# HGRN2 attention and a three-way maxout FFN on one core: the first FFN group started on half of its tokens, with its first weights on GpSimd's queue

## The chip, the cores and the metric

One Trainium2 chip, one core of it. The metric is device time in microseconds for one execution of the whole kernel (attention and FFN in one program). Times are medians over several runs; the profile is of one further execution.

## The reference

The reference is two blocks in a row. The attention block is a gated linear recurrence over 768 time steps, for 4 batches of 8 heads of width 48; the FFN works on the 3072 resulting tokens of width 384.

```python
f = 1.0 / (1.0 + np.exp(-f_logit))
for t in range(S):                       # S = 768
    state = f[:, :, t, :, None] * state + np.einsum('bhd,bhe->bhde', k[:, :, t], v[:, :, t])
    y[:, :, t] = np.einsum('bhd,bhde->bhe', q[:, :, t], state)
x = y.transpose(0, 2, 1, 3).reshape(B * S, H * D)          # 3072 x 384
h = np.maximum(np.maximum(x @ w1, x @ w2), x @ w3)         # 384 -> 768, three times
out = h @ w_out                                            # 768 -> 384
```

q, k, v and f_logit are fp32. The four FFN weights are fp64 in the reference and reach the kernel as 64-bit words, so the kernel turns each weight into fp32 itself.

## The kernel before

**Attention.** The recurrence is cut into chunks of 64 steps. A unit `u` is one chunk of two batches, 128 tokens, and there are NU = 24 units; `u` and `u + 2` are successive chunks of the same two batches, with a carried state `st`. The work of a unit is split over small functions that the program calls in an order written out by hand:

- `sigmoids(u)`: f is transposed on TensorE (line 243) and ScalarE writes `gate` (line 260).
- `after(u)`: VectorE's backward scan of the gates gives `r` (line 282), k is transposed (line 243), `kh` = k times r (line 289); GpSimd keeps the chunk's total decay in `ends` (line 288).
- `before(u)`: the forward scan gives `prod` (line 296), q is transposed, `qh` = q times prod (line 300).
- `carry(u)`: GpSimd decays the old state (line 306).
- `keys(u)`: TensorE transposes `kh` (line 315), ScalarE copies it to `ks` (line 317).
- `pairs(u)`: the 64x64 scores (line 328), masked by VectorE into `at` (line 331).
- `values(u)`: scores times v (line 342), keys times v (line 351), and the new state `st` on VectorE (lines 357 and 359).
- `finish(u)`: the carried state's part (line 372); ScalarE copies the result into `heads` (line 378).

The first BY_ROWS = 8 units are loaded with tokens on partitions, two DMAs of 64 partitions for each of f, k, q and v (line 159); later ones in 32x32 blocks (line 174). Pads of the tiles have fixed values, for f the value GATE_PAD.

**From attention to FFN.** Four units are one group of 512 tokens. `heads` has a head on 48 of 64 partitions; `pack` (line 389) moves the heads to dense feature rows of `xT` with DMAs inside the chip, 10 for a range of units. It can use SyncE's queue alone (`one`) or SyncE's and ScalarE's in turn (`both`).

**FFN.** For each of NJ = 6 slices j of 128 hidden features and each of the three input weights i, three matmuls of 512 tokens (line 401) fill a PSUM tile `p` (two buffers, shared with `busy` and with some early transposes); i = 0 is copied by ScalarE into `top` (line 405), i = 1 and i = 2 are folded in by VectorE (line 407), the last one into `hm`. Then, for each 128 tokens, six matmuls of 384 columns with `w_out` (line 422), a ScalarE copy (line 427) and two output DMAs (line 431). There are six such groups. `ffn` is a generator: `fill(n)` runs n of its steps (18 and then 4 of them), and the program places these calls between the parts of the attention units, so that TensorE always has FFN matmuls to do in between.

**Weights.** The weights come as 24 pieces of 384 KB: 18 of w1, w2, w3 in the order j, i and six of w_out. `load_weights` (line 200) loads a piece into `raw`, which has 12 buffers. Each piece is converted in three stages: `round_begin` (ScalarE, lines 212 and 215), `round_middle` (VectorE, lines 224 and 225, then GpSimd, line 227) and `round_end` (VectorE, line 234). Five pieces are begun before the first group; during the first group each FFN step runs one or two more.

**The start.** The program loads units 0 to 3, works through their attention, packs all 512 tokens at once (`pack(0, GRP - 1, xT, both)`), and starts `ffn(0)`. `busy(n)` issues n matmuls of 256 columns whose results nobody reads (line 448); `busy(14)` stands between the last part of unit 3 and the first FFN matmul.

**The end.** A test that the fast path was numerically allowed (`least`, lines 578 to 582) is worked out during the last group, between two of its steps. If it fails, another path (`general`) runs; it doesn't run here.

## Time and profile before

| | us |
|---|---|
| median of 4 runs | 487.1 |
| lowest and highest | 486.51, 490.26 |
| the profiled execution: device time | 491.23 |
| the profiled execution: span from first to last instruction | 489.5 |
| mean granted TensorE clock in it | 0.985 of full |

| engine | busy us | share of the span |
|---|---|---|
| TensorE, matmul (PE) | 468.2 | 96% |
| TensorE, weight load (PEld) | 253.4 | 52% |
| VectorE (DVE) | 223.3 | 46% |
| ScalarE (ACT) | 109.3 | 22% |
| GpSimd (POOL) | 99.3 | 20% |

A line of the profile names the line of the kernel, the engine, the operation, `out<-in` with the program's tile names, and the shapes. SPq, ACTq and DVEq are the issuing of instructions by an engine's sequencer, DMAs above all. An fp32 matmul or weight load stands as two records, one for each of two passes. In a timeline, a start and a duration are followed by the number of records merged; in brackets stand the idle time of the engine just before and what ended it. In the row of 40 slices a digit is the busy share of a slice of 12.2 us in tenths. The profiled execution lies 0.85% above the median (491.23 against 487.1).

### The profile page before, as it was taken

What the parts mean: (1) busy time and instruction counts of PE and PEld (TensorE: products, weight loads), DVE (VectorE), ACT (ScalarE), POOL (GpSimd) and SP (SyncE); (2) the same over time, 40 slices, a digit from 0 to 9 for tenths busy, and PEclk for the clock granted to TensorE, in tenths of its full rate; (3) what the DMA queues carried; (4) which work ended last, traced back from release to release, by engine and by line L of the source; (5) the groups of instructions that cost most, each with busy time, mean ns of one, the idle gap of its engine ahead of it and who ended that gap; (6) DMA issues with size and microseconds to landing.
All of it is one profiled execution on the core that took longest, in us unless ns stands there. A gap on an engine that the chain in (4) does not pass through costs nothing.

```text
span 489.5 us, 10037 instructions
## 1 busy us (share of the span) xinstructions
PE 468.2 (96%) x4101; PEld 253.4 (52%) x4101; DVE 223.3 (46%) x346; ACT 109.3 (22%) x227; POOL 99.3 (20%) x132
## 2 busy tenths in 40 slices
PE   5879999998999999999999999999999999989994
PEld 4656455555554556554456554456554445434452
DVE  7954999993263461353462253471354420112110
ACT  2344445332122122122022122022121011100000
POOL 2122456553110220211220211210211300000000
PEclk9979999998999999999999999999999999999998
DMA  9898999633664032566033575023630012100002
GB/s 128 134 234 200 261 214 206 91 75 66 112 87 63 1 66 50 94 95 88 1 68 58 100 91 74 0 64 67 106 45 1 1 48 50 32 1 1 0 20 51
DMA packets 170007, 38.51 MB, mean 79 GB/s; under 512 B 154976, under 2 KB 168800, under 8 KB 169952
## 3 DMA queue, kind: packets, MB, share of 16 engines
q1 hardware_dynamic: 166208, 36.50, 41.7%
q10 hardware_dynamic: 3744, 1.28, 1.4%
q8 instruction: 34, 0.56, 0.5%
q14 instruction: 21, 0.17, 0.1%
HBM read 28.31 MB, written 4.72 MB: 67 GB/s over the span
## 4 chain that ended last, share of the span: by engine, by line
PE 86%; SPq 6%; DMA 3%; DVE 1%; issue 1%; ACT 1%; POOL 0%; ACTq 0%; DVEq 0%; POOLq 0%
PE p L401 55%; PE p L422 19%; SPq L159 3%; PE y L342 2%; PE y L372 2%; SPq L174 2%; DMA v_ld<-in_v_dram 2%; PE a L328 2%; PE p L448 2%; PE y L351 2%; PE tr L315 1%; DMA k_ld<-in_k_dram 1%; PE tr L243 1%; SPq L389 1%; SPq L200 1%
## 5 line engine op out<-in xcount | busy, mean ns | idle before, releaser
L401 PE MATMUL p<-xT,w_in 128*128 128x512 f32 x648 | 288.1, 596 | 0.7 <-ACT top L405 0.7
L401 PEld LDWEIGHTS p<-xT,w_in 128*128 128x128 f32 x648 | 120.0, 190 | 138.4 <-issue 132.3
L422 PE MATMUL p<-w_out,hm 128*128 128x384 f32 x288 | 98.3, 497 | 0.6 <-DVE w_out L234 0.6
L407 DVE TENSOR_TENSOR top<-p,top 128x512 f32<-128x512 f32 x36 | 24.7, 686 | 119.2 <-PE p L401 119.0
L422 PEld LDWEIGHTS p<-w_out,hm 128*128 128x128 f32 x288 | 54.6, 193 | 39.0 <-issue 4.1
L405 ACT COPY top<-p 128x512 f32<-128x512 f32 x36 | 21.1, 586 | 179.8 <-PE p L401 179.8
L407 DVE TENSOR_TENSOR hm<-p,top 128x512 f32<-128x512 f32 x36 | 24.8, 689 | 50.5 <-PE p L401 50.5
L288 POOL COPY ends<-r 128x8 f32<-128x8 f32 x24 | 4.6, 192 | 190.2 <-DVE r L282 190.1
L227 POOL TENSOR_TENSOR top_bits<-top_bits,rest_bits 128x384 uint32<-128x384 uint32 x24 | 28.2, 1175 | 40.5 <-DVE top_bits L225 23.9
L427 ACT COPY o<-p 128x384 f32<-128x384 f32 x24 | 11.4, 476 | 107.7 <-PE p L422 104.5
L296 DVE TENSOR_TENSOR_SCAN prod<-gate,from_inv 128x520 f32<-128x520 f32 x24 | 34.7, 1448 | 0.0
L282 DVE TENSOR_TENSOR_SCAN r<-gate,from_one 128x520 f32<-128x520 f32 x24 | 30.9, 1288 | 3.1 <-issue 2.3
L378 ACT COPY heads<-y 64x256 f32<-64x256 f32 (+1 forms) x72 | 26.5, 368 | 10.4 <-PE y L372 9.2
L331 DVE TENSOR_TENSOR at<-a,mask 128x512 f32<-128x512 f32 x24 | 16.5, 687 | 24.9 <-PE a L328 24.9
L300 POOL TENSOR_TENSOR qh<-qt,prod 128x512 f32<-128x512 f32 x16 | 18.8, 1175 | 39.0 <-DVE qt L247 39.0
L342 PEld LDWEIGHTS y<-at,v_ld 64*64 64x64 f32 x768 | 13.8, 134 | 17.9 <-issue 14.1
L289 POOL TENSOR_TENSOR kh<-kt,r 128x512 f32<-128x512 f32 x16 | 19.7, 1231 | 14.1 <-DVE kt L247 13.4
L317 ACT COPY ks<-tr 128x512 f32<-128x512 f32 x22 | 12.8, 582 | 39.2 <-PE tr L315 38.9
L306 POOL TENSOR_TENSOR state<-st,ends 128x384 f32<-128x384 f32 x22 | 20.3, 923 | 0.2
L342 PE MATMUL y<-at,v_ld 64*64 64x64 f32 x768 | 17.3, 224 | 2.5 <-DMA v_ld<-in_v_dram 2.2
L247 DVE STREAM_TRANSPOSE gate<-sig 128x512 f32<-128x512 f32 x16 | 11.3, 706 | 17.6 <-ACT sig L263 17.6
L359 DVE TENSOR_TENSOR st<-y,state 128x384 f32<-128x384 f32 x20 | 11.1, 555 | 14.0 <-PE y L351 13.8
(66 smaller groups left out, 289.5 us busy)
## 6 DMA issues: line engine op xcount, KB each, us to landing
raw<-in_moe_w_dram SPq DMA_DIRECT2D x18, 384.0 KB, 6.2
v_ld<-in_v_dram SPq DMA_DIRECT2D x48, 96.0 KB, 3.1
out_dram<-o SPq DMA_DIRECT2D x48, 96.0 KB, 2.2
raw<-in_moe_w_out_dram SPq DMA_DIRECT2D x6, 384.0 KB, 6.2
xT<-heads SPq DMA_DIRECT2D x30, 72.0 KB, 2.1
f_ld<-in_f_logit_dram SPq DMA_DIRECT2D x32, 64.0 KB, 2.7
k_ld<-in_k_dram SPq DMA_DIRECT2D x32, 64.0 KB, 2.6
q_ld<-in_q_dram SPq DMA_DIRECT2D x32, 64.0 KB, 2.5
```

The source lines that it names most:

```text
L227: nc.gpsimd.tensor_tensor(top, top, rest, op=ALU.add)
L282: nc.vector.tensor_tensor_scan(r[:, 0:LEN][:, ::-1], flat(gate)[:, ::-1], flat(from_one)[:, ::-1], 1.0, op0=ALU.mult, op1=ALU.max)
L289: (nc.vector if u < BY_ROWS else nc.gpsimd).tensor_tensor(kh.rearrange("p h a t -> p a h t"), kt, by_batch(r[:, 1:LEN + 1].rearrange("p (x ...
L296: nc.vector.tensor_tensor_scan(flat(prod), flat(gate_tiles[u % 2]), flat(from_inv[u % 2]), 1.0, op0=ALU.mult, op1=ALU.max)
L300: (nc.vector if u < BY_ROWS else nc.gpsimd).tensor_tensor(qh, qt, by_batch(prod[:, :, 1:]), op=ALU.mult)
L306: nc.gpsimd.tensor_tensor(t, states[u % 2], ends[:, u, :].unsqueeze(2).to_broadcast([128, 2 * HP, D]), op=ALU.mult)
L342: nc.tensor.matmul(y[o:o + DP, a, hp * C:(hp + 1) * C], lhsT=v_ld[s, 2 * hp + par, :], rhs=d["at"][s, par, hp, :], start=(hp == 0), stop=F ...
L378: nc.scalar.copy(heads[o, :, t0 + a * C:t0 + (a + 1) * C], y[i, a, 0:HP * C].rearrange("p (h t) -> p h t", h=HP))
L401: nc.tensor.matmul(p, lhsT=w_in[i][:, kt, j * 128:(j + 1) * 128], rhs=xT[:, kt, :], start=(kt == 0), stop=(kt == NK - 1))
L405: nc.scalar.copy(top, p)
L407: nc.vector.tensor_tensor(hm[:, j, :] if i == 2 else top, p, top, op=ALU.max)
L422: nc.tensor.matmul(p[:, 0:DM], lhsT=hm[:, j, i * UT:(i + 1) * UT], rhs=w_out[:, j, :], start=(j == 0), stop=(j == NJ - 1))
```

## The change

The change has these parts:

1. `ffn(0)` takes its first two slices (j = 0, 1) in two halves: six steps on tokens 0 to 255 (units 0 and 1), then six steps on tokens 256 to 511, then j = 2 to 5 on all 512 as before. `xT` of group 0 is laid out as two halves. A half step yields once and a full step twice, so all `fill` counts are doubled.
2. `pack` is called twice for group 0, after unit 1 and after unit 3, both times on SyncE's queue alone; the loads of f and k of unit 4 stand between the two. `busy(14)` is gone.
3. The first nine weight pieces are loaded from GpSimd's queue, 3 + 3 + 1 + 1 + 1; piece 9 and later ones from SyncE's. The rounding runs at another pace (`ahead`), with `round_end` last.
4. f, k and q of units 0 to 7 are loaded by one DMA of 128 partitions, where the two batches alternate by partition; the transposes write PSUM with a stride to undo this. Loads of units 0 and 1 are spread over SyncE and ScalarE.
5. `after` is split: the scan is now `scan(u)` and is called earlier; `before(n)` moves ahead of a `fill`, next to `after(n)`. The state copies of units 0 and 1 go to ScalarE.
6. Pads of f are 0 and no longer rewritten by GpSimd between row and block layout (12 memsets less, line 144); instead the test at the end leaves pad rows out with `is_feature`, and its last part moves three full steps further down.

```diff
-            def load_weights(count, done=0):
+            def load_weights(count, done=0, queue=nc.sync):
...
-                    nc.sync.dma_start(out=dst, in_=src.rearrange("(a p) c -> p a c", a=a))
+                    queue.dma_start(out=dst, in_=src.rearrange("(a p) c -> p a c", a=a))
...
                     if u < BY_ROWS:
-                        load_tokens(rows[nm][u % 4], src, u, queues)
+                        c, bp = divmod(u, 2)
+                        queues[NAMES.index(nm) % 2].dma_start(
+                            out=rows[nm][u % 4][:, :, 0:D],
+                            in_=src[2 * bp:2 * bp + 2, :, c * C:(c + 1) * C, :].rearrange("b h t d -> t b h d"))
...
-            def transposed(x, name="tr"):
-                t = {"tr": ps_tr, "p": ps_f}[name].tile([128, HP, 128], FP32, name=name)
-                flat = x.rearrange("t h d -> t (h d)")
+            def transposed(nm, u, name="tr"):
+                t = {"tr": ps_tr, "p": ps_f}[name].tile([128, HP, 2, C], FP32, name=name)
                 for hp in range(HP):
-                    nc.tensor.transpose(t[:, hp, :], flat[:, hp * 128:(hp + 1) * 128], ident)
-                return t.rearrange("p h (a t) -> p h a t", a=2)
+                    nc.tensor.transpose(t[:, hp].rearrange("p a t -> p t a"), slots[nm][u % 4][:, hp * 128:(hp + 1) * 128],
+                                        ident)
+                return t.rearrange("p h a t -> p a h t")
...
                     if u < 2:
-                        nc.vector.tensor_copy(new, ds)
+                        nc.scalar.copy(new, ds)
...
+            def by_halves(xT):
+                return xT.rearrange("p k t -> p (k t)").rearrange("p (two k t) -> p two k t", two=2, k=NK)
...
-            def pack(u0, u1, xT, queues=one):
+            def pack(u0, u1, xT, queues=one, half=None):
                 t, n = slice(u0 * UT, (u1 + 1) * UT), 0
+                to = xT[:, :, t] if half is None else by_halves(xT)[:, half]
...
+                steps = [(j, slice(0, TOK)) for j in range(NJ)]
+                if g == 0:
+                    steps = [(j, slice(n * HALF, (n + 1) * HALF)) for n in range(2) for j in range(J_HALF)] + steps[J_HALF:]
+                done, n_step = 2, 0
+                for j, t in steps:
...
                         if g == 0:
-                            step, last = 3 * j + i, 3 * NJ
-                            for r in range(*(3 + (len(pieces) - 3) * n // last for n in (step, step + 1))):
-                                round_end(r)
+                            n_step += 1
+                            ahead = n_step + 2 if n_step <= 6 else 8 + (2 * n_step - 11) // 3 if n_step <= 12 else 12 + (n_step - 12) * 6 // 5
+                            for r in range(done, min(ahead, len(pieces))):
                                 if r + 2 < len(pieces):
                                     round_begin(r + 2)
-                                    round_middle(r + 2)
-                            load_weights(2, r + 1)
-                            next(pads, None)
+                                if r + 1 < len(pieces):
+                                    round_middle(r + 1)
+                                round_end(r)
+                                done = r + 1
+                            load_weights(2, done)
                         yield
+                        if w == TOK:
+                            yield
```

The order at the start after the change, from unit 2 on:

```python
scan(2)
after(2)
load_weights(3, queue=nc.gpsimd)
pairs(1)
finish(0)
carry(2)
before(2)
sigmoids(3)
busy(2)
values(1)
keys(2)
scan(3)
after(3)
pairs(2)
finish(1)
carry(3)
load_weights(3, queue=nc.gpsimd)
pack(0, 1, xT, one, 0)
load(GRP, one, "fk")
before(3)
busy(2)
for n in range(2):
    round_begin(n)
values(2)
keys(3)
finish(2)
round_middle(0)
load_weights(1, queue=nc.gpsimd)
pairs(3)
busy(2)
round_begin(2)
round_middle(1)
load_weights(1, queue=nc.gpsimd)
round_end(0)
values(3)
nc.tensor.transpose(ps_tr.tile([128, 128], FP32, name="tr"), ident, ident)
round_middle(2)
load_weights(1, queue=nc.gpsimd)
round_end(1)
finish(3)
round_begin(3)
pack(2, 3, xT, one, 1)
load_weights(3)
load(GRP, one, "q")
load_v(GRP)
load(GRP + 1)
load_v(GRP + 1)
pending.append(ffn(0, xT))
fill(6)
sigmoids(GRP)
scan(GRP)
after(GRP)
```

## The prediction

> **What bounds the kernel now.** I read the slices first, for where TensorE is not full; then busy time by window; then the timelines of the first 48 us, because everything the change touches lies there.
>
> ```profile
> PE   5879999998999999999999999999999999989994
> DVE  7954999993263461353462253471354420112110
> PEclk9979999998999999999999999999999999999998
> ```
>
> TensorE is at 9 in nearly all slices from the fourth on, and VectorE at 9 from the fifth to the ninth. The windows put numbers to that (columns after the window: its length, then busy us and count for PE, PEld, DVE, ACT, POOL, then clock, DMA share, GB/s):
>
> ```profile
> 42.30:105.00 62.70, 62.70 (x654) 34.16 (x652) 56.46 (x96) 29.45 (x62) 34.08 (x37) 1.00 0.86 185
> 105.00:130.00 25.00, 23.03 (x186) 13.46 (x187) 11.49 (x17) 4.19 (x9) 8.23 (x11) 0.93 0.45 83
> 150.00:432.00 282.00, 282.00 (x2420) 147.35 (x2418) 109.63 (x150) 52.37 (x109) 44.11 (x52) 1.00 0.32 54
> 432.00:436.00 4.00, 2.70 (x9) 1.14 (x8) 1.25 (x4) 0.00 (x0) 0.00 (x0) 1.00 0.00 0
> ```
>
> From 42.3 us on TensorE has no gap except 1.97 us after 105, 0.68 after 130, 1.30 at 432 and the last six. All of its work after 42.3 stays in the changed kernel. So a gain can come from three places only: FFN matmuls that run before 42.3, these gaps, nothing else. VectorE's 56.46 of 62.70 us says what stands next to TensorE in the first group: it turns weights there.
>
> Before 42.3, TensorE's timeline and those of its suppliers:
>
> ```profile
> 30.38 1.05 PE L342 MATMUL y<-at,v_ld 64*64 64x64 f32 x30 [2.24 <-DMA v_ld<-in_v_dram]
> ...
> 33.01 1.10 PE L372 MATMUL y<-qh,state 48*48 48x64 f32 x32 [0.34 <-DVE st L359]
> 34.05 8.37 PE L448 MATMUL p<-from_one,ident 128*128 128x256 f32 x28
> 42.26 2.74 PE L401 MATMUL p<-xT,w_in 128*128 128x512 f32 x6
> ```
>
> ```profile
> 34.18 1.14 ACT L378 COPY heads<-y 128x256 f32<-128x256 f32 x3 [3.98 <-PE y L372]
> 35.35 3.20 ACTq L389 DMA_DIRECT2D xT<-heads  x5
> ```
>
> ```profile
> 34.96 4.83 SPq L389 DMA_DIRECT2D xT<-heads  x5
> ...
> 99.79 6.29 SPq L389 DMA_DIRECT2D xT<-heads  x10
> ```
>
> Unit 3 waits 2.24 us for v. Its result is in `heads` at 35.3; the ten packing DMAs are issued until 39.8 and land some 2.4 us later; FFN starts at 42.26. The 8.37 us of L448 fill that hole with useless matmuls. The last line is a packing on SyncE alone: 0.63 us a DMA.
>
> VectorE's last lines before the group, and the first scan in it:
>
> ```profile
> 32.87 1.49 DVE L234 SCALAR_TENSOR_TENSOR w_in<-raw,top_bits 128x384 uint32<-128x384 uint32 x3
> 39.19 0.36 DVE L224 TENSOR_SCALAR top_bits<-top_bits 128x384 f32<-128x384 f32 x1 [4.83 <-ACT top_bits L212]
> ...
> 46.10 0.36 DVE L224 TENSOR_SCALAR top_bits<-top_bits 128x384 f32<-128x384 f32 x1 [4.12 <-ACT top_bits L212]
> ...
> 47.04 2.06 DVE L282 TENSOR_TENSOR_SCAN r<-gate,from_one 128x520 f32<-128x520 f32 x1 [0.18 <-ACT gate L260]
> ```
>
> It idles 9 us between 34 and 46, then is full to 109. This idle time is what an earlier start can use.
>
> **What the skill says.** The Trainium skill, "DMA: Bandwidth & Descriptors", section "SWDGE vs HWDGE vs iDMA": DMAs from GpSimd have their descriptors computed by GpSimd's own cores, so each such issue stands in the same queue as the weight additions of L227. First-byte latency is given there (Specifications) as about 1 us against 0.6 from SyncE. No run here shows a GpSimd issue; the same transfer costs SyncE 0.57 us (L200, median). "SBUF — State Buffer", "A bandwidth-pool intuition that's wrong", gives about 620 ns for one alone and 3100 ns when a two-port VectorE copy locks it out. "TensorE: Matmul & The Clock Gate", Part 1: idle stretches of about 3.4 us halve the clock. The trace agrees in kind: the clock is 0.64 and 0.67 at 30 to 40 us, after the wait for v.
>
> **The change, part by part.**
>
> *Attention of units 0 to 3.* VectorE's chain runs at 3.9, 4.6, 4.6 and 4.5 us a unit (start to start). The first two state copies (0.56 each) go to ScalarE, with a 0.67 us wait, -1.6 us in all over two copies and the wait. The first f now comes as one DMA of twice the size, which I put at +0.3: unit 3's `qh` ends at 24.5 instead of 25.8. The loads stop mattering: SyncE issues 26 DMAs of 0.63 us and three weight pieces before v of unit 3 goes out by 25.1; after, 9 double ones (0.63 to 1.26 each) and 6 of 0.63 stand ahead, so v is issued by 16 us at the latest, and the 2.24 us wait goes. Then `st` 25.0, L372 25.5, L328 26.1, `at` 26.8, L342 and L351 27.9, `st` 28.5, L372 29.4, three `heads` copies (1.14): 30.5 against 35.3.
>
> *Packing.* The second half: 10 DMAs x 0.62 = 6.2 on one queue instead of about 4.5 on two, then 2.3 to land: 39.0, against 42.2. The first half: `heads` of unit 1 is there at 22.5 (23.05 before, less the copies), + 6.2 + 2.3 = 31.0. SyncE is free for both; f and k of unit 4 go out between them, near 30, and are wanted at 39. q of unit 4 falls behind the second packing and three weight pieces: issued near 39, it lands near 43, when the steps below want it.
>
> *Weights on GpSimd.* The first nine issues stand in POOL's order before the fourth L227: 3 after `ends` of unit 2 (16.8), 3 after the `state` of unit 3, then one after each addition. With d us per issue the fourth addition ends at 16.8 + 9d + 1.9 (two `state`, one `ends`) + 4 x 1.1 = 23.1 + 9d. d lies between 0.6 and 3.1 by the two prices above; I take 1.0: at 32.1. Weights 0 to 5 are then ready at 27.5, 29.5, 32, 33.5, 35 and 36.5.
>
> *Half steps.* Twelve of 3 matmuls x 2 passes. A 512-column pass costs 0.43 us (2.58 for six), 256 columns half of it, since a transpose of 128 columns with its own load costs 0.11 a pass, so the load hides: 1.29 a step, nothing added. VectorE pays 8 half folds instead of 4 full, about +0.4. From 31.2 six half steps run to 39.0, kept up by the weights above; then the second half is there. Thus 7.7 us of FFN are done by 39.0, and the start lies 42.3 - 31.3 = 11 us ahead. The clock may drop again after the wait before 31 and cost up to 3.4 us in these steps; the wait that follows covers it.
>
> *What is late next.* ScalarE's order puts L212 of piece 9 in the sixth half step, ahead of unit 4's sigmoid. Piece 9 comes from SyncE after the second packing: issued at 37.3, landing 3.9 to 6.2 later (minimum and median of `raw`), say 42. Then 1.0 for L212 and L215 and 0.6 for the gate: 43.6, not much before 47.04. VectorE, in order, waits there for the scan. After it come scan 1.25, reciprocal 0.2, L289 0.6, two L224/L225 0.7, L234 0.55, and only then the fold that frees `p` of half step 8: 47.3. Step 10 waits for it; step 11 waits for the next fold, behind L296 and L300: 49.5. Step 12 ends at 52.1. Done by then: 15.5 of FFN and 1.3 of transposes, 16.8. The old kernel has done 52.1 - 42.3 = 9.8. The lead is 7.0 us: 4 of the 11 are given back.
>
> *The rest of the group.* VectorE needs about 49.5 us from that scan to the last L234: 4 units at 5.6 less one `at` and `st`, 5.2 of folds, 16 x 0.55, 15 x 0.95 for L224/L225 with their delays behind POOL; that is 93. TensorE reaches the last `w_out` piece at 107.8 - 7 = 101. VectorE holds the lead, with 8 us in hand. The 1.41 us wait of unit 8's L328 (for POOL's `qh`) may stay: `before(8)` is earlier, but one fill less stands between. I take no change, -1.4 to +2.
>
> *Edits at nothing.* Strided PSUM writes of transposes: same column count, 0; if they cost double, 48 x 0.11 = 5.3 us on the path from unit 4 on. Fewer pads on GpSimd: 12 x 0.52 off the path. The test at the end: three full steps hide its wait, -1.3 (the gap at 432).
>
> *Sum.* -7.0 - 1.3 = -8.3. Against the profiled execution: 491.2 - 8.3 = 482.9, span 481.2. That execution stood 4.1 us above the median, so against the median: 487.1 - 8.3 = **478.8**.
>
> **Rivals.** A change under 1% (4.9 us) is about what a measurement can't tell from none.
>
> - *The stall eats the lead.* If piece 9 lands after 8.5 us (the longest `raw`), the gate is at 47.3 and step 12 at 55.8: lead 3.3, sum -4.6, 482.5. With transposes at double cost as well, 487. For it: 4 us are lost there even with my landing. Against: the packing's slow traffic should be over by then.
> - *GpSimd's issues end it (the slower case).* The place is POOL's queue between `ends` of unit 2 and the fourth L227. Half step 6 ends at 27.2 + 9d; the old kernel has done 7.7 us of FFN-stage work at 50. Break-even at d = 2.5 us; with the test's 1.3 us, over 1% slower from d = 3.2. At d = 3.5: -8.7 + 1.3, 494.5. For it: VectorE's two-port operations in that stretch. Against: there are six of 0.36 us, and 3.2 lies above the dearer price.
> - *No stall, and more.* Piece 9 lands early, unit 8's wait goes too: -11 - 1.3 - 1.4, 473.4.
>
> **How the numbers follow.** Forecast (475 to 482) 0.60; stall 0.18; slower 0.10; more 0.12. The range 473 to 489 leaves out the slower case and a little of each end. Faster by over 1% (below 482.2): 0.60 + 0.12 and a small part of the stall, 0.74; within 1%: 0.15; slower: 0.11.
>
> **What would show it.** No L448 run before the FFN; the first half-width L401 near 31 and the next six near 40; POOL issues of `raw` of about 1 us each; a VectorE idle stretch of some 4 us ahead of unit 4's scan, with the scan near 43.6; TensorE idle 2 to 4 us in half steps 9 to 11; the last `w_out` piece some 7 us earlier; no wait at the test. The prediction is wrong if POOL issues pass 2.5 us, if half-width passes cost over 0.25 us, or if full-width steps after the twelfth wait for folds.

## The result, and the profile after

| | before | after |
|---|---|---|
| median | 488.58 us (55 runs) | 486.77 us (34 runs) |
| lowest and highest | 485.94, 491.73 | 485.03, 489.38 |
| profiled execution | 491.23, span 489.5 | 487.39, span 485.7 |

The ratio is 0.9965, with a 95% interval of 0.995 to 0.998: a gain of about 0.4%, or 1.7 to 1.8 us, where 8.3 us were forecast. Executions of both kernels spread with the granted TensorE clock (of the kernel before, one at a mean clock of 0.999 took 486.0 us and one at 0.982 took 491.3), and the profiled execution of the kernel before lies near the slow end, so the two profiled executions differ by more than the medians: by 3.84 us. The sums below are made between these two; about half of what they add up to is not in the medians.

The slices after:

```profile
PE   5978899899999999999999999999999999999994
PEclk9959999999999999999999999999999999999999
```

PEclk falls to 5 in the third slice, 24 to 36 us, and TensorE is at 8 in the fourth and fifth, where FFN now runs. The windows there (busy us of PE, PEld, DVE, ACT, POOL, then clock, DMA share, GB/s):

```profile
25.00:30.00 5.00, 3.53 (x80) 3.00 (x84) 1.09 (x3) 0.25 (x2) 0.00 (x0) 0.59 1.05 275
30.00:35.00 5.00, 5.00 (x120) 4.05 (x116) 1.87 (x5) 2.57 (x6) 3.44 (x4) 0.50 0.51 135
```

The clock is about half for ten microseconds, and the DMA engines are full until 30. TensorE's timeline shows where it starts and what it leads to:

```profile
26.80 1.01 PE L351 MATMUL y<-at,v_ld 64*64 64x64 f32 x26 [1.26 <-DMA v_ld<-in_v_dram]
...
36.94 2.86 PE L430 MATMUL p<-xT,w_in 128*128 128x256 f32 x12
...
42.04 1.56 PE L430 MATMUL p<-xT,w_in 128*128 128x256 f32 x6 [0.32 <-DVE w_in L240]
...
51.79 0.63 PE L249 MATMUL tr<-ident,q_ld 128*128 128x128 f32 x4 [0.79 <-DMA q_ld<-in_q_dram]
...
56.76 2.86 PE L430 MATMUL p<-xT,w_in 128*128 128x256 f32 x12 [1.18 <-DVE hm L437]
59.45 0.60 PE L324 MATMUL tr<-ident,kh 128*128 128x128 f32 x4
```

The first FFN matmul is at 36.94, not 31. Half steps 3 to 6 start at 40.19, 42.04, 43.98 and 46.01: 1.94 us apart on average, each released by VectorE's line 240 (which finishes a weight piece), where the work of one is 1.3. Half steps 9 to 12 wait three times, 2.3 us in all.

The last line is the anchor (a point of equal work) that I use for all kernels below: the keys of unit 4, which follow half step 12. The kernel before takes these keys earlier in its order, but it has done the same amount of TensorE work at 42.26 + 15.5 (six full steps) + 1.3 (three sets of transposes) = 59.1. At this point the changed kernel has no lead at all, 59.1 - 59.45 = -0.35. ScalarE and SyncE in the same stretch:

```profile
37.06 1.14 ACT L387 COPY heads<-y 128x256 f32<-128x256 f32 x3 [4.02 <-PE y L381]
...
47.66 0.58 ACT L218 ACTIVATE top_bits<-raw 128x384 f32<-128x384 f32 x1 [1.85 <-DMA raw<-in_moe_w_dram]
```

```profile
22.56 10.31 SPq L403 DMA_DIRECT2D xT<-heads  x10
...
37.84 6.30 SPq L403 DMA_DIRECT2D xT<-heads  x10
```

Unit 3 is in `heads` at 38.2, later than in the kernel before (35.3). The first packing takes 10.31 us of issuing, the second 6.30.

What gain there is comes later. From TensorE's timeline, the kernel before and then after:

```profile
108.33 1.56 PE L422 MATMUL p<-w_out,hm 128*128 128x384 f32 x4 [0.55 <-DVE w_out L234]
...
112.33 0.69 PE L328 MATMUL a<-qh,kh 48*64 48x64 f32 x32 [1.41 <-POOL qh L300]
112.96 9.70 PE L422 MATMUL p<-w_out,hm 128*128 128x384 f32 x24
```

```profile
87.63 0.66 PE L381 MATMUL y<-qh,state 48*48 48x64 f32 x32 [1.51 <-DVE st L368]
...
112.79 8.01 PE L456 MATMUL p<-w_out,hm 128*128 128x384 f32 x24
...
125.78 7.89 PE L430 MATMUL p<-xT,w_in 128*128 128x512 f32 x18
```

The last line is the second anchor, the first matmul of FFN group 1; before it is at 127.64. So from a lead of -0.35 us at the first anchor it goes to +1.86 at the second. On that stretch the kernel before loses 0.55 (a wait for `w_out` at 108), 1.41 (unit 8's wait for `qh`) and 1.69 (the same 24 records in 9.70 instead of 8.01, at a low clock), and the changed one 1.51 (the wait for `st` at 87): 3.65 - 1.51 = 2.14. After it come 0.68 (the wait before at 149) and 1.30 (the test at 432), both gone. 1.86 + 0.68 + 1.30 = 3.84, the whole difference of the two profiled executions. None of it is a lead of TensorE that the early FFN start left at half step 12. What the early start left is on VectorE: its last weight piece ends at 102.2, in the kernel before at 108.7, and the wait for `w_out` is gone.

### The profile page after: what moved, and what is told of

Same layout as the page of the kernel before. It is cut to its first block, busy times and chain, and to the rows that moved or that the text cites. A ratio compares the mean times of both kernels' runs of the same rounds, so it can differ in the third digit from the quotient of the medians.

```text
span 485.7 us, 10050 instructions
## 1 busy us (share of the span) xinstructions
PE 464.2 (96%) x4117; PEld 256.1 (53%) x4117; DVE 216.2 (45%) x341; ACT 110.4 (23%) x231; POOL 113.1 (23%) x133
## 4 chain that ended last, share of the span: by engine, by line
PE 86%; DVE 5%; SPq 4%; DMA 2%; ACT 1%; issue 1%; DVEq 0%; ACTq 0%
PE p L430 54%; PE p L456 19%; PE y L351 3%; PE y L381 3%; PE a L337 2%; PE y L360 2%; SPq L171 2%; SPq L161 2%; DMA v_ld<-in_v_dram 2%; PE tr L324 2%; DVE top_bits L230 1%; DVE w_in L240 1%; DVE r L287 1%; DVE prod L305 1%; PE tr L249 1%
## 5 line engine op out<-in xcount | busy, mean ns | idle before, releaser
L430 PE MATMUL p<-xT,w_in 128*128 128x512 f32 (+1 forms) x684 | 289.9, 575 | 3.0 <-DVE w_in L240 1.6
L430 PEld LDWEIGHTS p<-xT,w_in 128*128 128x128 f32 x684 | 126.3, 190 | 137.3 <-issue 123.7
L456 PE MATMUL p<-w_out,hm 128*128 128x384 f32 x288 | 96.3, 489 | 0.0
L437 DVE TENSOR_TENSOR top<-p,top 128x512 f32<-128x512 f32 (+1 forms) x38 | 24.9, 657 | 133.4 <-PE p L430 133.4
L435 ACT COPY top<-p 128x512 f32<-128x512 f32 (+1 forms) x38 | 21.4, 562 | 176.1 <-PE p L430 176.1
L297 POOL COPY ends<-r 128x8 f32<-128x8 f32 x24 | 7.5, 311 | 209.5 <-DVE r L287 205.0
L437 DVE TENSOR_TENSOR hm<-p,top 128x512 f32<-128x512 f32 (+1 forms) x38 | 24.7, 651 | 41.1 <-PE p L430 41.0
L298 POOL TENSOR_TENSOR kh<-kt,r 128x512 f32<-128x512 f32 x16 | 31.5, 1966 | 17.4 <-DVE kt L254 17.4
L305 DVE TENSOR_TENSOR_SCAN prod<-gate,from_inv 128x520 f32<-128x520 f32 x24 | 30.1, 1254 | 0.0
L387 ACT COPY heads<-y 64x256 f32<-64x256 f32 (+1 forms) x72 | 26.5, 369 | 11.7 <-PE y L381 10.5
L326 ACT COPY ks<-tr 128x512 f32<-128x512 f32 x22 | 12.8, 583 | 43.6 <-PE tr L324 43.4
L254 DVE STREAM_TRANSPOSE gate<-sig 128x512 f32<-128x512 f32 x16 | 11.4, 711 | 25.1 <-ACT sig L269 25.1
L381 PE MATMUL y<-qh,state 48*48 48x64 f32 x704 | 15.1, 225 | 2.0 <-DVE st L368 1.9
```

The costliest lines, as they stand in the source:

```text
L298: (nc.vector if u < BY_ROWS else nc.gpsimd).tensor_tensor(kh.rearrange("p h a t -> p a h t"), kt, by_batch(r[:, 1:LEN + 1].rearrange("p (x ...
L305: nc.vector.tensor_tensor_scan(flat(prod), flat(gate_tiles[u % 2]), flat(from_inv[u % 2]), 1.0, op0=ALU.mult, op1=ALU.max)
L381: nc.tensor.matmul(y[o:o + D, a, hp * C:(hp + 1) * C], lhsT=st[r, a, hp, :], rhs=d["qh"][r, a, hp, :], start=False, stop=(hp == HP - 1), s ...
L387: nc.scalar.copy(heads[o, :, t0 + a * C:t0 + (a + 1) * C], y[i, a, 0:HP * C].rearrange("p (h t) -> p h t", h=HP))
L430: nc.tensor.matmul(p if g or w < TOK else p.rearrange("p (two t) -> p two t", two=2), lhsT=w_in[i][:, kt, j * 128:(j + 1) * 128], rhs=rhs, ...
L435: nc.scalar.copy(top, p)
```

## The experiments

"Lead" is the time by which a kernel's profiled execution passes an anchor ahead of that of the kernel before (59.1 and 127.64). Each ratio is to the runs of the kernel before that were made with that row, so ratios compare better than times; 0.001 is 0.5 us.

| kernel | median, us | ratio to before, 95% interval | lead at keys of unit 4 | lead at group 1 |
|---|---|---|---|---|
| the change | 486.77 | 0.9965 [0.995, 0.998] | -0.4 | 1.9 |
| e1 weights behind the loads | 486.67 | 0.9969 [0.9952, 0.9987] | 0.5 | 2.7 |
| e2 no addition | 485.94 | 0.9942 [0.9924, 0.996] | 0.4 | 3.1 |
| e3 clock bridged | 485.59 | 0.9947 [0.9927, 0.9966] | 1.3 | 3.5 |
| e4 weights on SyncE | 488.52 | 0.9992 [0.9972, 1.0013] | -1.4 | 0.9 |
| e5 no half start | 492.55 | 1.0071 [1.005, 1.0091] | -1.4 | -3.3 |
| e6 before, later edits | 488.4 | 0.9989 [0.9971, 1.0007] | | 1.1 |
| e7 e3 and q early | 486.46 | 0.9945 [0.9912, 0.9979] | 0.8 | 3.0 |
| e8 e7, both queues | 494.28 | 1.0104 [1.0066, 1.0143] | -5.3 | -3.6 |
| e9 e7 and light pace | 485.81 | 0.9953 [0.9933, 0.9973] | 2.0 | 3.0 |
| e10 e1, q early, light pace, bridge | 486.55 | 0.9961 [0.9943, 0.9979] | 1.5 | 2.5 |
| e11 e9 and before(n) late | 485.14 | 0.9927 [0.9911, 0.9943] | 2.7 | 4.5 |
| e12 e11 and piece 9 late | 486.64 | 0.9964 [0.9946, 0.9982] | 3.9 | 1.1 |
| e13 e12 and less conversion | 483.08 | 0.9878 [0.9827, 0.993] | 3.6 | 7.4 |
| e14 e12 and even pace | 485.62 | 0.9935 [0.9913, 0.9957] | 4.9 | 4.8 |

By these intervals only e11 and e13 are faster than the change, and only e5 and e8 slower; the others overlap with it, e4 and e14 just so.

A lead comes from one execution, and part of it is chance. e12 and e14 do the same up to the first anchor and stand at 3.9 and 4.9 there; e9 and e11 also do, at 2.0 and 2.7. The difference lies ahead of the half steps: in the middle of unit 3's `values`, TensorE stands idle for 0.7 to 2.7 us in e9 to e14, and the profile names nothing that it waits for. From half step 1 to the first anchor e9 and e11 both take 22.1 us, e12 and e14 both 19.6. And since the kernel before loses 3.65 us between the anchors, a kernel that waits nowhere there gains that much.

The theories at the start: (A) the attention of units 2 and 3 is late because v comes late and the clock then halves; (B) the packing's transfers are late in their own right; (C) GpSimd's descriptor work costs; (D) the conversion of weights, with GpSimd's addition against VectorE's operations, sets the pace of the half steps.

### The attention: e1 and e3

e1 puts the first weight loads behind those of the units:

```diff
                 after(2)
-                load_weights(3, queue=nc.gpsimd)
                 pairs(1)
...
                 carry(3)
-                load_weights(3, queue=nc.gpsimd)
+                load_weights(6, queue=nc.gpsimd)
                 pack(0, 1, xT, one, 0)
```

begins the rounding of pieces 0 and 1 after `finish(2)`, and takes `pairs(3)` ahead of its second stage. 

> The changed kernel, but no weight is loaded before the attention loads are out: GpSimd issues the first six weight DMAs together after the state of unit 3 (near 21 us instead of 16.7), and the first two conversions begin after unit 2's finish. Theory A (the weights' DMAs share the engines with the last loads, v of unit 2 lands late, TensorE's clock halves in the gap, and unit 3 runs at half speed): v of unit 2 lands by 24.5, no wait at its L351, clock above 0.9 from 25 to 35, unit 3's heads copies near 31 instead of 37.1, first half step near 33; 2 to 4 us faster than the changed kernel, ratio to the kernel before 0.988 to 0.992. Theory B (the first packing on SyncE's queue alone, 10.3 us long, sets the first half step): heads copies come earlier but the first half step stays at 36 or later, ratio 0.995 to 0.998 as in the changed kernel.

The wait for v is gone, the clock holds until 30, and `heads` of unit 3 starts at 32.06 instead of 37.06. But the time hardly moves, because the first half step then waits for the packing. Its ten issues still take 7.07 us, and a packing DMA takes 6.7 us (median) from issue to landing, where 2.4 was the median in the kernel before. After these waits the clock is at 0.50 between 35 and 40:

```profile
35.58 7.15 PE L430 MATMUL p<-xT,w_in 128*128 128x256 f32 x20 [0.99 <-DMA xT<-heads]
```

e3 leaves v late and only keeps the clock up over the wait:

```diff
                 before(3)
-                busy(2)
+                busy(9)
```

> The changed kernel with nine instead of two unused matmuls ahead of unit 2's L351, so that TensorE is busy while v of unit 2 is on its way. Theory A (the gap halves the clock, and half the clock delays unit 3): clock 1.0 from 25 to 35; unit 3's heads copies start near 33 instead of 37.1; first half step near 35; 1 to 3 us faster than the changed kernel, ratio 0.990 to 0.995. Rival (unit 3 is late for v alone and for VectorE's order; the clock costs nothing): heads copies within 1 us of 37, ratio 0.995 to 0.998.

The clock is 1.0 from 25 to 50, and the first half step is at 34.29 instead of 36.94. So of the 5 us that e1 found in the attention, 2.65 are the clock, as far as one profiled execution of each can tell; the ratios differ by 0.9 us, and their intervals overlap. Half steps 3 to 6 are still 1.94 apart, and then a transfer takes part of the lead:

```profile
50.46 1.04 PE L249 MATMUL tr<-ident,q_ld 128*128 128x128 f32 x4 [2.09 <-DMA q_ld<-in_q_dram]
```

Theory A holds for the attention; B stands behind it, as e1 shows.

Why is v late? The DMA view of 4 to 42 us (KB of one, median us from issue to landing), before and then after:

```profile
v_ld<-in_v_dram SPq DMA_DIRECT2D x9, 96.0 KB, 4.2
```

```profile
v_ld<-in_v_dram SPq DMA_DIRECT2D x8, 96.0 KB, 7.9
```

v of unit 3 is issued by 20.9 us, 4 us earlier than before (25.1), though not by 16 as forecast: of the 96 KB issues ahead of it, one took 2.60 us instead of 0.63. The DMA engines are full from 4 to 30 us, at some 160 GB/s up to 18 us, and v lands later after its issue, 7.9 instead of 4.2 us. In e1 and in e4, where the first weights go out behind v, TensorE does not wait for v of unit 2.

### The queue of the weights: e4

At the same five places:

```diff
-                load_weights(3, queue=nc.gpsimd)
+                load_weights(3, queue=nc.sync)
...
-                load_weights(1, queue=nc.gpsimd)
+                load_weights(1, queue=nc.sync)
```

> The changed kernel with the first nine weight DMAs on SyncE's queue instead of GpSimd's, at the same places in the program. Theory A (what matters is that the weights run beside the last loads, not which engine issues them): SyncE's order puts the first three behind v of unit 3, so they start near 21 instead of 16.7; v of unit 2 lands earlier, the clock stays up longer, but the single ones fall behind the first packing (after 30), so conversions 6 to 8 come later; time within 2 us of the changed kernel, either side, ratio 0.992 to 1.000. Theory C (GpSimd's descriptor work is what costs: 9 x 0.76 us in the queue of its additions): conversions come earlier with SyncE and the kernel is 3 us or more faster, ratio below 0.990.

1.3 us slower than the change by the ratios (1.75 by the medians), the intervals just touching. Six pieces delay the first packing's issue from 22.56 to 24.84, but that is not where the time goes: v is in time, and half step 1 starts at 35.26, even earlier than in the change. Three more pieces stand before the second packing, which is issued until 45.3 instead of 44.1; the half steps are level with the change at the sixth (46.18 against 46.01), and then q of unit 4, behind that packing, is waited for 1.94 us instead of 0.79. So GpSimd's queue doesn't hurt and seems to help a little, and its price was even below my estimate (0.76 to 0.82 us an issue). Theory C falls.

### The conversion loop: e2

Without line 233 the weights lack their last bits.

```diff
-                    nc.gpsimd.tensor_tensor(top, top, rest, op=ALU.add)
```

> The changed kernel without GpSimd's addition in the conversion of the weights (L233): the low bits are left out of all 24 pieces. Theory A2 (each conversion is a loop of 1.94 us, 1.18 us of GpSimd's addition and 0.76 of VectorE's two-port operations that can't run beside it, and this paces the half steps): the half steps 3 to 6 start 1.3 to 1.5 us apart instead of 1.9, L230 takes 0.36 everywhere, step 6 ends about 2.5 us earlier, and the first FFN group ends 3 to 5 us earlier; ratio to the kernel before 0.986 to 0.992. Rival (the pace comes from ScalarE's L218 and L221 or from the landing of the weights): the starts stay 1.9 apart and the time stays within 1 us of the changed kernel, ratio 0.995 to 0.998.

This is the loop in the changed kernel, GpSimd and then VectorE:

```profile
43.60 1.18 POOL L233 TENSOR_TENSOR top_bits<-top_bits,rest_bits 128x384 uint32<-128x384 uint32 x1 [0.76 <-DVE top_bits L231]
```

```profile
43.84 1.16 DVE L230 TENSOR_SCALAR top_bits<-top_bits 128x384 f32<-128x384 f32 x1
45.03 0.36 DVE L231 TENSOR_SCALAR top_bits<-top_bits 128x384 uint32<-128x384 uint32 x1
45.31 0.55 DVE L240 SCALAR_TENSOR_TENSOR w_in<-raw,top_bits 128x384 uint32<-128x384 uint32 x1
```

The addition runs from 43.60 to 44.78; line 230 of the next piece starts under it and ends 0.22 after it: 1.16 us instead of 0.35. Only then comes line 231, and then the next addition. The two take turns: 1.18 + 0.76 = 1.94 us a piece. The Trainium skill states this in "SBUF — State Buffer", "Who interferes with whom": a VectorE `tensor_scalar` in a two-port mode and a GpSimd operation exclude each other, and the later one waits in full. The trace agrees to about 0.1 us: 0.35 after the addition's end would be 45.13, and line 230 ends at 45.00. Without the addition line 230 takes 0.35 or 0.36 in all half steps to 49, and half steps 4 to 6 are one block:

```profile
43.30 4.32 PE L429 MATMUL p<-xT,w_in 128*128 128x256 f32 x18 [0.55 <-DVE w_in L239]
```

Some 1.4 us apart. Theory D holds for the pace. The time fell by only 0.8 us by the medians (1.1 by the ratios, with intervals that overlap): what had been hidden behind VectorE, q of unit 4, is waited for next, 1.82 us at 52.9.

### What the parts of the change are worth: e5 and e6

e5 takes out the half start and keeps the rest.

```diff
-                pack(0, 1, xT, one, 0)
...
-                pack(2, 3, xT, one, 1)
+                pack(0, GRP - 1, xT, both)
+                busy(14)
```

> The changed kernel with the half start taken out: group 0 begins on all 512 tokens, packed once on both queues after unit 3, with the 14 filling matmuls of the kernel before in front; loads, weight queue, scan order and the test stay changed. If the half start as built is still worth something, this costs what it saved: heads(3) stays near 35 to 37, packing on two queues 4.5 and 2.3 to land, first FFN matmul near 43 to 44, against 42.3 in the kernel before; full steps of 2.6 us leave the conversion of a piece (1.9) no way to hold them up, so the lead at the keys of unit 4 should be about 1.5 us below that of the changed kernel: about 488.3. Rival: the conversion loop and the waits of half steps 9 to 12 had eaten the half start whole, and this is equal to the changed kernel, 486.8 within 0.7.

492.55: the half start is worth 5.2 us within the change by the ratios (5.8 by the medians), and the other edits without it cost 3.9 against the kernel before. Against the change I had expected a loss of 1.5, and why it is more is instructive. At the keys of unit 4 the loss is only 1.1 us; the rest comes later, first here:

```profile
63.46 0.69 PE L337 MATMUL a<-qh,kh 48*64 48x64 f32 x32 [2.32 <-DVE qh L309]
```

and then in a clock of 0.91 between 60 and 80. The half steps are of use less for TensorE than for VectorE: `ffn` carries the conversion, so an earlier FFN step is an earlier piece of VectorE's work. In e5 VectorE stands idle for 8.29 us, until 47.62, before the first of these steps, and it ends its last piece at 107.3 instead of 102.2. (e5 also packs on both queues, so it is not the half start alone: its first FFN matmul is at 42.51, and TensorE waits for that packing once more until 44.56.)

e6 is the kernel before with the later order edits only: `scan(n)` ahead of the fill, `before(n)` next to `after(n)`, the test's last part three steps down.

```diff
                         sigmoids(n)
+                        scan(n)
...
                         after(n)
+                        before(n)
...
-                        before(n)
                         carry(n)
...
-                fill(8)
+                fill(6)
...
+                fill(3)
                 n_low = ps_tr.tile([1, 1], FP32, name="tr")
```

> The kernel before with only the later order edits: scan called before the fill, before(n) next to after(n), and the last part of the end test three full steps further down. If the measured gain of the change comes from the later edits (1.30 at the test, and unit 8's wait of 1.41), this gains 1.3 to 2.7 us against the kernel before: 485.9 to 487.3, ratio 0.9945 to 0.9973. Rival: it comes from the start; then only the test's 1.3 is seen, or nothing because the earlier scan delays folds in the first group: ratio 0.998 to 1.000.

Not separable from no change: the rival. The 1.41 at unit 8 and the 1.30 at the test are gone, but VectorE gives it back:

```profile
108.91 2.54 PE L428 MATMUL p<-w_out,hm 128*128 128x384 f32 x4 [2.03 <-DVE w_out L234]
```

### One limit behind the other: e7 to e11

e7 adds to e3 that q of unit 4 is loaded with f and k, ahead of the second packing.

```diff
-                load(GRP, one, "fk")
+                load(GRP, one, "fkq")
...
-                load(GRP, one, "q")
```

> The changed kernel with two edits: nine filling matmuls instead of two ahead of values(2), as in the earlier run that kept the clock at 1.0, and q of unit 4 loaded next to f and k of unit 4, ahead of the second packing instead of behind it. If q behind the packing is what holds half steps 9 to 12 once the clock is kept, its 2.09 us wait is gone, the keys of unit 4 come near 55.8 and the time is 2 us below the run with the filling matmuls alone: about 483.6. Rival: piece 9, still behind the second packing on SyncE, makes ScalarE and so the gate of unit 4 late, and the wait only changes its name: 485.0 to 485.8.

The wait for q is gone and others stand in its place, this one and 1.20 us at 55.65:

```profile
52.89 1.56 PE L430 MATMUL p<-xT,w_in 128*128 128x256 f32 x6 [1.58 <-DVE top L437]
```

The rival was right: ScalarE waits 4.60 us for piece 9, the gate of unit 4 comes at 48.73, and VectorE, idle 2.18 us for it, has its folds late.

e8 adds two edits to e7.

```diff
-                    nc.vector.tensor_scalar(top.bitcast(FP32), top.bitcast(FP32), HI_MIN, None, op0=ALU.max)
+                    nc.vector.scalar_tensor_tensor(top.bitcast(FP32), top.bitcast(FP32), HI_MIN, top.bitcast(FP32),
+                                                   op0=ALU.max, op1=ALU.max)
...
-                pack(2, 3, xT, one, 1)
+                pack(2, 3, xT, both, 1)
```

> The kernel of the run with q early, with two more edits: line 230 as a scalar_tensor_tensor (same values, not a two-port operation, priced 0.55 like line 240 instead of 0.35), and the second packing on SyncE's and ScalarE's queues in turn. If the exclusion between GpSimd's addition and VectorE's two-port operations sets the 1.94 us a piece, the pace of half steps 3 to 6 falls by at most 0.4 us each, and the second packing's issue takes some 4.8 instead of 6.3 us: about 1.5 us below that run, 482.1. Rival: line 231, still two-port, is excluded just the same and the pace stays 1.9; only the packing helps, if at all: 0 to 0.7 below it.

Slower than the kernel before, by 1.0%. ScalarE's timeline:

```profile
36.53 6.32 ACTq L404 DMA_DIRECT2D xT<-heads  x4
42.89 0.37 ACT L436 COPY top<-p 128x256 f32<-128x256 f32 x1 [6.05 <-DMA xT<-heads]
```

Four packing DMAs take 6.32 us to issue, and the copy of the third half step's fold stands behind them in ScalarE's order; TensorE waits 5.91. Putting the second packing on SyncE alone, which I had priced as a loss of 1.7 us of issue time, keeps ScalarE free for the half steps. The other edit fails too: the new form of line 230, which has two inputs in SBUF (the same tile twice), takes 1.02 to 1.35 beside the addition, and a piece takes 2.13.

e9 adds to e7 a lighter pace: one piece finished in half steps 7 to 12 instead of four.

```diff
-ahead = n_step + 2 if n_step <= 6 else 8 + (2 * n_step - 11) // 3 if n_step <= 12 else 12 + (n_step - 12) * 6 // 5
+ahead = n_step + 2 if n_step <= 6 else 8 + max(0, n_step - 8) // 4 if n_step <= 12 else 9 + (n_step - 12) * 5 // 4
```

> The kernel of the run with q early, with one more edit: during half steps 7 to 12 one weight piece is finished instead of four (they are needed only from full step 4 on), the other three later, 1.25 a full step instead of 1.2. If VectorE, which stands at 4.83 and 4.76 busy of 5 us between 50 and 60, is what holds half steps 9 to 12 (1.58 and 1.20 us of waits there for the folds), three pieces of about 1.3 us less shorten these waits by 2 to 3 us: the keys of unit 4 near 55.8, no new wait in the full steps (VectorE has 3 us free between 60 and 80), the time 2.3 below that run: 484.2. Rival: VectorE carries a backlog all along, and what is put off comes back as a wait for w_out at 104 or for st before: equal to that run, 486.4 (its profiled execution 484.7 of span).

The waits for folds fall to 0.45 and 0.71, the keys of unit 4 come 1.2 us earlier than in e7, and these 1.2 us are lost again before group 1, at `w_out` (0.26, 0.53) and at unit 8's `kh` (0.74): both kernels lead by 3.0 there, as the rival said. What is left near 49 is the prediction's own stall, for which VectorE stands idle 1.90 us:

```profile
48.23 0.56 ACT L218 ACTIVATE top_bits<-raw 128x384 f32<-128x384 f32 x1 [4.32 <-DMA raw<-in_moe_w_dram]
```

e10 joins e1, q early, the lighter pace, and one line more:

```diff
+                busy(7)
                 pending.append(ffn(0, xT))
```

> The changed kernel with the first weights put behind the loads (as in the first run), q of unit 4 with f and k of unit 4, the lighter pace of weights in half steps 7 to 12, and 7 filling matmuls right ahead of the first half step, in the hole in which the first packing is waited for. In that first run v was in time, heads of unit 3 stood at 32.06, but the first half step waited for the packing and ran at half clock from 35 to 40. If the clock was the rest of it, half step 1 starts near 35 at full clock, and half steps follow at 1.9; half step 6 ends near 45.5, the keys of unit 4 stand near 56.5: 484.5. Rival: the pace of 1.94 a piece sets half step 6 whatever the clock is, and as the conversion began later with the later weights nothing is gained against the first run: 486.7.

It stands at e1's time. The filling matmuls run to 37.3, past the 35.6 at which the packing had landed in e1, and half steps 4 to 6 keep their pace of 1.9 to 2.0: the rival.

e11 changes e9:

```diff
                         after(n)
-                        before(n)
+                        if n >= BY_ROWS:
+                            before(n)
...
                     values(u)
                     if n < NU:
+                        if n < BY_ROWS:
+                            before(n)
                         carry(n)
```

> The kernel of the run with the lighter pace, with one edit more: for units 5 to 7 before(n) is called after values(u), as in the kernel before, not next to after(n). In the changed kernel st of unit 5 comes behind the second scan and qh on VectorE and TensorE waits 1.51 us for it at 87. If that order is the cause, this wait goes and nothing else comes: 1.5 below that run. Rival: the order only moves the wait to pairs(n), which then waits for qh of unit n: within 0.7 of that run.

The wait for `st` near 84 is gone, and none for `qh` comes in its place. But in e9 that wait was only 0.46 us, no longer the 1.51 of the change, so 1.5 could not come of it. The median is 0.7 us better than e9's, the edge of what the rival allowed, with intervals that overlap.

### The whole of the conversion: e12, e13, e14

e12 begins piece 9 in half step 9, so that it no longer stands before the gate of unit 4 on ScalarE; after half step 12 it finishes 1.5 pieces a full step.

```diff
-ahead = n_step + 2 if n_step <= 6 else 8 + max(0, n_step - 8) // 4 if n_step <= 12 else 9 + (n_step - 12) * 5 // 4
+ahead = n_step + 2 if n_step <= 5 else 7 + n_step // 9 if n_step <= 12 else 8 + (n_step - 12) * 3 // 2
```

> The kernel of the run with before(n) late, with one more edit of the pace: piece 9 is begun in half step 9 instead of half step 6, so that ScalarE's line 218 on it no longer stands ahead of the gate of unit 4; after half step 12 one and a half pieces a full step instead of one and a quarter. In the run with the lighter pace ScalarE waited 4.32 us for piece 9's transfer, which stands behind the second packing, the gate came at 49.14 and VectorE stood idle 1.90 us for it. If that order is the stall that the prediction named, the gate of unit 4 comes near 46 (after its f is transposed), the half steps 9 to 12 lose some 0.5 us instead of 1.8, the keys of unit 4 stand near 55: 1.5 below the run with before(n) late, 483.6, ratio 0.990. Rival: VectorE or q stands behind it and the lead goes back at w_out near 105, where line 240 already holds TensorE for 0.53: 485.1, ratio 0.9927.

The stall that the prediction named is gone, and half steps 7 to 12 have no wait at all. And yet the time is worse than e11's:

```profile
49.95 5.45 PE L430 MATMUL p<-xT,w_in 128*128 128x256 f32 x24
...
83.63 0.67 PE L381 MATMUL y<-qh,state 48*48 48x64 f32 x32 [1.82 <-DVE st L368]
85.82 1.13 PE L337 MATMUL a<-qh,kh 48*64 48x64 f32 x32 [1.52 <-DVE qh L309]
```

The lead of 3.9 us is spent at 83 to 86, where `st` and `qh` stand behind conversions on VectorE (`st` starts at 82.93, right after three pieces), and in the clock of 0.86 between 80 and 105.

e13 takes line 233 and line 230 out of e12 (weights without their last bits and the guard for very small values); e14 keeps all the work and spreads it evenly, one and a third pieces a step.

```diff
-                    nc.vector.tensor_scalar(top.bitcast(FP32), top.bitcast(FP32), HI_MIN, None, op0=ALU.max)
...
-                    nc.gpsimd.tensor_tensor(top, top, rest, op=ALU.add)
```

> The kernel with piece 9 late, without two of the five operations on a weight piece: GpSimd's addition (line 233) and VectorE's line 230 (the weights then lack their last bits' rounding and the guard for very small values). VectorE's work per piece falls from 1.26 us and what the addition holds it up (0.5 to 0.8) to 0.91. If VectorE's conversion as a whole limits the first group, the lead of 4 us at the keys of unit 4 (55.2) grows to 6 or 7 (half steps 3 to 6 also faster), is kept to group 1, the waits of 1.82 and 1.52 at 83 to 86 and the clock of 0.86 are gone, and the time is 479 to 481.5. Rival: the lead is lost to something else, the DMAs of the raw pieces or the attention's own chain between units; then waits of 2 us or more stay between 60 and 105 and the time is 484 to 486.

```diff
-8 + (n_step - 12) * 3 // 2
+8 + (n_step - 12) * 4 // 3
```

> The kernel with piece 9 late, with the pace after half step 12 spread evenly: one and a third pieces a full step instead of one and a half. VectorE then has 18 pieces less work ahead of st and qh of unit 6 at 83 than before by about two pieces (2 x 1.5 us): if only the uneven pace caused the waits of 1.82 and 1.52 us there and the fall of the clock after them, they go, the lead of 4 us stays to about 105 and some 0.5 to 1 us is lost at w_out: 482.9, ratio 0.988. Rival: VectorE's whole conversion limits the group; the same 2 to 3 us are then waited for at w_out near 103 to 107: 485, ratio 0.9925 like the run with before(n) late.

e14's lead reaches group 1, after waits of 1.47 at 82.91 (for `qh`), 0.42 and 0.53 at `w_out`, and 0.73 at unit 8's `kh`. By the ratios it is 1.5 us better than the change, e11 1.9, with intervals that overlap: nearer the rival's 485 than the 482.9 expected, and no gain over e11 is shown.

In e13 there is no wait above 0.2 us between the first half step and 130:

```profile
80.00:105.00 25.00, 25.00 (x306) 14.08 (x305) 20.31 (x35) 10.67 (x23) 3.51 (x5) 1.00 0.50 79
```

Its first six half steps run through in 10.0 us without a wait, and its lead goes from 3.6 to 7.4: it loses nothing where the kernel before loses 3.65. That of e12, with the same order and pace, fell to 1.1, and by the ratios e13 is 4.2 us faster than e12. So the conversion work of VectorE and GpSimd bounds the first group. Which of the two operations counts how much is not separated; without the addition alone (e2) the gain was 1.1. The time lies 1.6 us above the upper end of what I had given: e13 starts half step 1 only at 36.45, after the longest of the unexplained idle stretches (2.72 us) and at a clock of 0.66 between 35 and 40.

## Why the prediction was wrong

The mechanism was named, and its signs hold: an earlier start, a part of it given back, a wait less at the test. Its one big term, the lead of 7.0 us at the end of the half steps, was -0.35, which is a miss of 7.35 us. By the steps below it splits into 5.7 us because half step 1 starts at 36.94 instead of 31.2, and 2.7 because the first six half steps take 10.5 instead of 7.8; the stretch to the end of half step 12 gives 1.0 back, 12.1 us instead of 13.1. So two steps failed: that the loads stop mattering for the attention, and that the half steps run at the pace of their own work.

| step | forecast | measured | settled by |
|---|---|---|---|
| unit 3 in `heads` | 30.5 | 38.2 | e1, e3 |
| first packing, issue | 6.2 | 10.31 | e1 (7.07, still late) |
| second packing, issue | 6.2 | 6.30 | |
| GpSimd, one issue | 1.0 | 0.76 to 0.82 | |
| a half step's work | 1.29 | 1.3 | |
| pace of half steps 3 to 6 | 1.29 | 1.94 | e2 |
| weights 0 to 5 ready | 27.5 to 36.5 | 33.6 to 45.9 | e2 |
| half step 1 starts | 31.2 | 36.94 | e1, e3 |
| half step 6 ends | 39.0 | 47.4 | |
| gate of unit 4 | 43.6 | 49.2 | e12 |
| waits in half steps 9 to 12 | 4 | 2.3 | e7, e9, e12 |
| last weight piece (VectorE) | 93 | 102.2 | e13 |
| test at the end | -1.30 | -1.30 | |

1. **The attention term failed first, by 7.7 us.** The step was: the loads stop mattering, since v is issued by 16. It was issued by 20.9 and landed 7.9 us after its issue. I read an issue queue, and the DMA engines behind it were the limit; new traffic (weights from 16.7 on) went into the same engines. The first packing had been issued by 32.9, and half step 1 did not wait for it: it stands behind unit 3 in TensorE's order. Then TensorE's gap, 2.75 us in two parts (1.49 and 1.26) around four matmuls, was followed by half the clock for 10 us. The prediction saw that the clock might drop and said that the following wait would cover it; e3 shows 2.65 us that nothing covered. How long the clock stays down is not fixed: in e5 a gap of 2.64 us in the same place was followed by 0.71 and 0.94 in the same two windows. The Trainium skill, "TensorE: Matmul & The Clock Gate", Part 1, speaks of about 3.4 us of idling; here a shorter broken gap was enough, as was the single wait of 2.24 in the kernel before.
2. **The first packing** was priced from a packing at 99.79 us, when the engines had a mean busy share of 0.27. Between 22 and 33, at a share of 0.92, the same ten issues took 10.31, and a DMA landed 5.6 us after its issue instead of 2.3. In the change this stood behind item 1; e1 shows it.
3. **The conversion was priced at 0.95 + 0.55 us a piece and then treated as hidden**, by a head start: the first weights ready 4 us before half step 1. They came 6 us later, because VectorE's first line 230 (29.34) stands in its order behind `st` of unit 2 (28.87), late with the attention. Without a head start the pace of the conversion shows, and that is 1.94, not 1.5. The delay behind GpSimd's additions was in my total for VectorE, but not in this loop, where the two take turns.
4. **The stall** that I named (ScalarE's line 218 on piece 9, behind the second packing) is real: 1.85 us here, 4.32 in e9. But in the change VectorE did not idle for it, as I had said: it was busy with its own backlog to 49.66 when the scan started. It did in e7 and e9 (2.18 and 1.90 us). Removing the stall (e12) shortened the half steps by 2.5 us and gave nothing in time until VectorE's work was lighter (e13).
5. **"VectorE holds the lead, with 8 us in hand" would have failed next.** It finished its last piece at 102.2, not 93; with no lead of TensorE left, `w_out` was wanted only at 105.9, so this cost the change nothing yet. But a lead of 4 us was given back in e12, and one of 4.9 was kept in e14 only with waits for `w_out`: no order of the same work got past it.
6. **Right:** GpSimd's issues don't decide (e4), half width and strided transposes cost nothing extra, the last weight piece some 7 us earlier (6.6), and 1.3 us at the end. None of the three signs that I had named for being wrong appeared: GpSimd's issues stayed under 1 us, a half-width pass took 0.22, and no full-width step waited for a fold. The rival "the stall eats the lead" comes nearest in microseconds, and its 487 with transposes at double cost (by its own sum 487.8) nearly hits the median, but that is luck: the transposes cost what they did. One reading was wrong without effect: the scans of VectorE's chain start 3.9, 5.7, 5.1 and 5.0 us apart; the 4.5 and 4.6 are without the state work and the wait.

What stays open: the last 0.5 us or so between e11, e14 and e3, whose intervals overlap; the idle 0.7 to 2.7 us of TensorE in unit 3, for which the profile names no cause; and what would remain if the loads themselves were smaller or in larger packets, which was not tried.

## What to carry to other kernels

Before moving a stage forward, sum the work of the engine that feeds it (here VectorE's 24 conversions) over the whole stretch up to the point where the stage ends: here a lead that this engine couldn't follow was given back at the next wait, wherever the order put it. Price a transfer by a row from the same stretch of time, not from a quiet one, and ask of every cleared queue what the engines behind it are doing. When an edit removes a wait and the time stays, follow an anchor further down (the same matmul in both kernels) until the lead is gone; the wait there is the next bound to look at.

## What the runs showed of the hardware that was not expected

- Beside GpSimd's addition (two SBUF tiles) VectorE operations of several kinds took longer: `tensor_scalar` 0.35 to 1.16 us, `scalar_tensor_tensor` with two SBUF inputs 0.55 to 1.35 (e8), a scan 1.24 to 2.04.
- A wait of TensorE of 1.49 us, four matmuls, and a wait of 1.26 us were followed by a clock of 0.50 to 0.59 for 10 us; nine matmuls of 256 columns in place of two in that hole (e3) kept it at 1.0. The single wait of 1.51 at 87 in the change left the clock at 1.00.
- The ten small DMAs of a packing took between 6.30 and 10.40 us to issue on one queue: 6.30 at a mean busy share of the DMA engines of 0.44 (the change's second packing), 7.99 at 0.75 and 10.40 at 0.92 (e3). Five of them on ScalarE's queue (e8) held up a later ScalarE copy by 6 us.
